# Band attention in pieces of 32 queries and 38 keys, with a unit's scores in one step and its sums over keys in another

## The chip, the cores and the metric

The kernel runs on one core of one Trainium2 chip. The metric is the device time of one execution in microseconds; times are compared as medians of several runs. The profile comes from one further execution that the hardware profiler recorded. TensorE (PE, with its weight loads as PEld) multiplies, VectorE (DVE), ScalarE (ACT) and GpSimd (POOL) do the rest, and SyncE (SP) issues the transfers.

## The reference

A block of attention feeds two feed-forward blocks. For each of 4 batches and 8 heads, of 576 positions and 64 channels, the attention is a sum of two softmaxes: one over the sequence averaged in fours (144 positions, its result repeated four times), and one over a band of seven keys around each query.

```python
q_d = q.reshape(B, H, Sd, factor, D).mean(axis=3)      # factor = 4; k_d, v_d alike
out_up = np.repeat(sm_attn(q_d, k_d, v_d), factor, axis=2)
mask = np.abs(pos[:, None] - pos[None, :]) < factor
scores = np.where(mask, scale * np.matmul(q, k.transpose(0, 1, 3, 2)), -1000000000.0)
attn = np.exp(scores - np.max(scores, axis=-1, keepdims=True))
attn = attn / (np.sum(attn, axis=-1, keepdims=True) + 1e-09)
x = out_up + np.matmul(attn, v)                         # to 2304 tokens x 512
x = (((x @ w1) * (x @ w2)) @ w3) @ w_out
h = x @ w_in;  out = (h / (1 + np.exp(-h))) @ moe2_w_out
```

## The kernel before

The work is one program for one core, written as Python loops that emit instructions; a scheduler may move an instruction on its engine past others that it does not depend on, so the order on an engine is near to the order in the code but not the same.

**Attention** is done in 16 units of two heads (one in partitions 0 to 63, the other in 64 to 127). A unit has these parts, and the letters are also the names of the tiles in the profile. D1 makes the scores of the averaged sequence (`sd`), D2 transposes the softmaxed ones (`td`), D3 multiplies by the averaged values (`od`, copied to `ods`). L1 makes band scores (`s`) in blocks of 64 queries and 70 keys, adds the mask into `E`, takes the maximum and the softmax; L2 transposes `E` (`tl`, copied to `ET` by ScalarE); L3 multiplies by the values in `vw` (`ol`), adds the averaged part (`xf`) and splits the sum into two float32r parts `x` (a cast on ScalarE and a difference on GpSimd or, in the opening, VectorE). Since a bank of PSUM holds 512 columns and nine blocks of 70 need 630, L1, L2 and L3 run twice a unit, for five blocks and for four (`BLOCKS`). These matmuls are plain float32; each appears as two MATMUL records in the trace, a transpose as one.

**The rest** works on float32 numbers split into two float32r parts, three matmuls for each product. In the opening, weights are loaded as 64-bit numbers (`st`), decoded (`dec`) and split, and w3 times w_out is formed (`wp`). Then, for eight pieces of tokens (320 and 256 a batch), `ab_group` makes the two gated products and `y_group` the output, which goes to DRAM. The second feed-forward block (`h`, `g`, `o`) takes the last third of the time.

**The order.** The steps of attention stand in a list `steps`; `run_steps(n)` runs them up to the n-th. In the opening a list of events with due times mixes them with the decoding and `wprime`; later one call after each slot (a slot is one `ab_group` or half a `y_group`, 12 matmuls on the whole array) lets a step or so go in. Before, a unit has nine steps, so that each of D1, L2, L1, L3, D2, L1, L2, D3, L3 stands between two slots:

```python
n = 36 + max(0, i - 3) if i < 40 else 72 + ((i - 39) * 36) // 46   # steps due after slot i
```

PSUM has four banks for `mm` tiles (`ab`, `y`, `wp`), two with the tag T (`td`, `tl`, `od`, `ol`) and two with the tag S (`sd`, `s`). `ab_group` of a batch reads `x` of its four units, the fourth unit's last. The built program gives each matmul the part of TensorE's 128x128 array that just holds its rows (32, 64 or 128) and output columns: 128x128 for `ab`, `y`, `td` and `tl`, 64x64 for `sd` and `s`, 128x64 for `od` and `ol`.

Of the kernel before, what the change touches and what calls it, by code (L numbers as in the profile page):

```python
# [19 lines left out]
QB, KW, NQB = 64, 70, 9  # L20
BLOCKS = ((0, 1, 2, 3, 4), (5, 6, 7, 8))
SD = S // 4
# [10 lines left out]
def tile_model(ctx: ExitStack, tc: tile.TileContext, qk, vw, vr, w12, w3t, wo, wb, out):  # L33
# [33 lines left out]
    mask = cst.tile([P, 6, KW], F32, name="mask")  # L67
    nc.gpsimd.memset(mask, 0.0)
    for e in range(2):
        mv = mask[64 * e:64 * e + 64]  # L70
        nc.gpsimd.affine_select(
            out=mv, in_=mv, compare_op=ALU.is_ge, fill=NEG, base=0,
            pattern=[[0, 6], [1, KW]], channel_multiplier=-1,
        )
        nc.gpsimd.affine_select(
            out=mv, in_=mv, compare_op=ALU.is_ge, fill=NEG, base=6,
            pattern=[[0, 6], [-1, KW]], channel_multiplier=1,
        )
    nc.gpsimd.memset(mask[:, 0, 0:3], NEG)
    nc.gpsimd.memset(mask[:, 5, KW - 3:KW], NEG)  # L80
# [103 lines left out]
    def load_vw(u):  # L184
        if u >= NU:
            return
        t = att.tile([80, NQB, P], F32, tag="vw", name=f"vw{u}", bufs=1)
        nc.sync.dma_start(t, vw[u // 4, u % 4])
        A["vw", u] = t
# [8 lines left out]
    def pool_qk(u):  # L198
        if u >= NU:
            return  # L200
        t = att.tile([P, 2, SD], F32, tag="qkd", name=f"qkd{u}", bufs=2)
        src = A["qk", u].rearrange("p (t c) -> p t c", t=2)[:, :, :S]
        src = src.rearrange("p t (s r) -> p t s r", r=4)
        nc.vector.tensor_reduce(out=t, in_=src, axis=AX.X, op=ALU.add)
        A["qkd", u] = t
# [10 lines left out]
    def softmax(src, E, m, n, width, scale, gain):  # L216

        z = att.tile([P, 16], F32, tag="sm", name="sm")
        nb, sv = z[:, 0:n], z[:, 8:8 + n]
# [97 lines left out]

    def L2(u, h):
        E = A.pop(("E", u, h))
        n = len(BLOCKS[h])  # L320
        ET = att.tile([KW, 5, P], F32, tag="ET", name=f"ET{u}_{h}")
        for j0, j1 in ((0, n // 2), (n // 2, n)):
            tp = t_tile(f"tl{u}_{h}_{j0}")
            for j in range(j0, j1):
                nc.tensor.transpose(tp[:KW, (j - j0) * P:(j - j0 + 1) * P], E[:, j, :], ident)  # L325
            nc.scalar.copy(
                ET[:, j0:j1, :].rearrange("p j q -> p (j q)"), tp[:KW, :(j1 - j0) * P]
            )
        A["ET", u, h] = ET
# [3 lines left out]
    def L3(u, h):  # L333
        ET = A.pop(("ET", u, h))
# [139 lines left out]
    events += [(0.2 + i, 2, i) for i in range(36)]  # L474
# [155 lines left out]
    for i, slot in enumerate(slots):  # L630
# [9 lines left out]
        run_steps(36 + max(0, i - 3) if i < 40 else 72 + ((i - 39) * 36) // 46)  # L640
# [141 lines left out]
```

## Time and profile before

| | |
|---|---|
| median of 3 runs | 947.56 us (945.53 to 948.35) |
| profiled execution | 947.99 us, span 946.2 us, mean granted TensorE clock 0.978 |
| TensorE, matmul / weight load | busy 892.4 us (94%) / 802.3 us (85%) |
| VectorE / ScalarE / GpSimd | busy 459.7 / 317.1 / 258.0 us |
| opening, 0 to about 172 us | TensorE waits in it, VectorE is the fullest engine |
| gated products with attention, to about 436 us | TensorE without gaps |
| gated products without attention, then the second block | TensorE nearly without gaps |

The span runs from the first to the last instruction. Busy time is the union of an engine's instructions; matmuls are pipelined and their ends modelled, so what a group costs is better read from the starts of its neighbours than from its own length.

### The profile page before, as it was taken

What the parts mean: (1) busy time and instruction counts of PE and PEld (TensorE: products, weight loads), DVE (VectorE), ACT (ScalarE), POOL (GpSimd) and SP (SyncE); (2) the same over time, 40 slices, a digit from 0 to 9 for tenths busy, and PEclk for the clock granted to TensorE, in tenths of its full rate; (3) what the DMA queues carried; (4) which work ended last, traced back from release to release, by engine and by line L of the source; (5) the groups of instructions that cost most, each with busy time, mean ns of one, the idle gap of its engine ahead of it and who ended that gap; (6) DMA issues with size and microseconds to landing.
All of it is one profiled execution on the core that took longest, in us unless ns stands there. A gap on an engine that the chain in (4) does not pass through costs nothing.

```text
span 946.2 us, 15978 instructions
## 1 busy us (share of the span) xinstructions
PE 892.4 (94%) x6224; PEld 802.3 (85%) x6224; DVE 459.7 (49%) x997; ACT 317.1 (34%) x966; POOL 258.0 (27%) x269
## 2 busy tenths in 40 slices
PE   5767789999999999999999998999999999999998
PEld 4545578899989999999999897989989989999897
DVE  7888999635453444324637999222221221222221
ACT  6466675443333333334224533211211211111111
POOL 1000014434243333324112154422422423322221
PEclk9787999999999999999999999999999999999999
DMA  8555544221422121121512544200200000000000
GB/s 272 167 179 182 185 132 127 63 76 56 139 78 77 58 72 53 31 68 40 178 65 75 185 139 133 63 6 1 68 1 1 34 1 1 34 1 1 35 1 34
DMA packets 26285, 73.58 MB, mean 78 GB/s; under 512 B 2912, under 2 KB 10080, under 8 KB 26208
## 3 DMA queue, kind: packets, MB, share of 16 engines
q1 hardware_dynamic: 26208, 72.54, 24.3%
q8 instruction: 49, 0.80, 0.4%
q14 instruction: 28, 0.23, 0.1%
HBM read 63.09 MB, written 9.44 MB: 77 GB/s over the span
## 4 chain that ended last, share of the span: by engine, by line
PE 73%; DVE 12%; DMA 6%; ACT 4%; issue 3%; POOL 1%; SPq 0%; DVEq 0%; ACTq 0%; POOLq 0%
PE o L697 19%; PE h L670 19%; PE ab L500 18%; PE y L533 9%; DVE dec L142 3%; DMA st<-wb 3%; DVE dec L147 2%; DMA st<-w3t 2%; PE ol L341 1%; PE s L300 1%; DVE dec L133 1%; DMA st<-w 1%; DVE dec L137 1%; PE tl L325 1%; ACT dec L123 1%
## 5 line engine op out<-in xcount | busy, mean ns | idle before, releaser
L681 POOL TENSOR_TENSOR g<-gf,g 128x384 fp32r<-128x384 f32 x96 | 104.8, 1092 | 275.9 <-DVE g L680 275.9
L678 DVE TENSOR_TENSOR gf<-h,sg 128x384 f32<-128x384 f32 x96 | 53.4, 556 | 258.7 <-ACT sg L676 258.7
L676 ACT ACTIVATE sg<-h 128x384 f32<-128x384 f32 x96 | 47.0, 491 | 290.3 <-PE h L670 290.3
L500 PE MATMUL ab<-x,w_wA 128*128 128x320 f32 (+1 forms) x768 | 112.7, 300 | 0.8 <-DVE w_wA L160 0.8
L500 PE MATMUL ab<-x,w_wB 128*128 128x320 f32 (+1 forms) x768 | 113.2, 300 | 0.0
L533 PE MATMUL y<-c,w_wC 128*128 128x320 f32 (+1 forms) x768 | 111.2, 299 | 0.0
L500 PEld LDWEIGHTS ab<-x,w_wA 128*128 128x128 f32 x768 | 103.2, 188 | 4.4 <-issue 2.0
L500 PEld LDWEIGHTS ab<-x,w_wB 128*128 128x128 f32 x768 | 103.6, 188 | 2.6 <-issue 0.8
L533 PEld LDWEIGHTS y<-c,w_wC 128*128 128x128 f32 x768 | 102.9, 188 | 2.7 <-issue 1.6
L518 POOL TENSOR_TENSOR c<-cf,c 128x320 fp32r<-128x320 f32 (+1 forms) x64 | 54.8, 856 | 140.2 <-DVE c L517 120.5
L407 PE MATMUL wp<-w_wA,w_w 128*128 128x512 f32 x192 | 63.4, 477 | 13.1 <-ACT w_w L159 12.0
L123 ACT ACTIVATE dec<-st 128x512 f32<-128x512 f32 x72 | 48.4, 674 | 69.9 <-DMA st<-wb 30.9
L224 ACT ACTIVATE E<-E,sm 128x70 f32<-128x70 f32 x144 | 49.0, 342 | 49.0 <-DVE sm L220 49.0
L407 PEld LDWEIGHTS wp<-w_wA,w_w 128*128 128x128 f32 x192 | 41.4, 228 | 24.9 <-ACT w_w L159 14.1
L514 DVE TENSOR_TENSOR cf<-ab,af 128x320 f32<-128x320 f32 (+1 forms) x64 | 29.0, 453 | 66.3 <-PE ab L500 60.1
L697 PE MATMUL o<-w_wA,g 128*128 128x512 f32 x216 | 55.7, 401 | 4.2 <-POOL g L681 3.6
L670 PE MATMUL h<-yhl,w_wC 128*128 128x384 f32 x288 | 55.2, 341 | 0.0
L670 PE MATMUL h<-yhl,w_wB 128*128 128x384 f32 x288 | 54.2, 337 | 0.5 <-ACT yo L542 0.5
L670 PE MATMUL h<-yhl,w_wA 128*128 128x384 f32 x288 | 54.4, 337 | 0.0
L697 PE MATMUL o<-w_wB,g 128*128 128x512 f32 x216 | 54.2, 395 | 0.0
L697 PE MATMUL o<-w_wC,g 128*128 128x512 f32 x216 | 54.1, 395 | 0.0
L670 PEld LDWEIGHTS h<-yhl,w_wC 128*128 128x128 f32 x288 | 52.0, 191 | 2.2
(92 smaller groups left out, 1377.6 us busy)
## 6 DMA issues: line engine op xcount, KB each, us to landing
st<-wb SPq DMA_DIRECT2D x32, 512.0 KB, 4.1
qk<-qk SPq DMA_DIRECT2D x16, 579.0 KB, 3.8
st<-w3t SPq DMA_DIRECT2D x16, 512.0 KB, 5.2
st<-w SPq DMA_DIRECT2D x16, 512.0 KB, 4.6
vw<-vw SPq DMA_DIRECT2D x16, 360.0 KB, 3.7
vr<-vr SPq DMA_DIRECT2D x16, 320.0 KB, 3.2
st<-ydram SPq DMA_DIRECT2D x12, 384.0 KB, 3.3
out<-os SPq DMA_DIRECT2D x18, 256.0 KB, 2.1
```

The source lines that it names most:

```text
L123: nc.scalar.activation(v.bitcast(F32), st[:, :, 1].bitcast(F32), AF.Abs)
L224: nc.scalar.activation(E[:, j, :], src[:, j, :], AF.Exp, bias=nb[:, j:j + 1], scale=scale, accum_out=sv[:, j:j + 1],)
L407: nc.tensor.matmul(acc, lhsT=w3v[:, a, k, j * P:(j + 1) * P], rhs=wov[:, b, k, :], start=(gp == 0 and k == 0 and n == 0), stop=(gp == 3 an ...
L500: nc.tensor.matmul(acc[:, :N], lhsT=wv[:, i, w, kk, :], rhs=x[:, j, :], start=(n == 0), stop=(n == 11),)
L514: nc.vector.tensor_tensor(out=cf, in0=acc[:, :N], in1=C.pop("af"), op=ALU.mult)
L518: nc.gpsimd.tensor_tensor(out=c[:, 1], in0=cf, in1=c[:, 0].bitcast(F32), op=ALU.subtract)
L533: nc.tensor.matmul(acc[:, :N], lhsT=WP[kf // 2][:, i, kf % 2, ec * P:(ec + 1) * P], rhs=c[:, j, :], start=(kf == 0 and n == 0), stop=(kf = ...
L670: nc.tensor.matmul(acc[:, :TT], lhsT=w[:, i, kk, :], rhs=y[:, j, kk, :], start=(n == 0), stop=(n == 11),)
L676: nc.scalar.activation(sg, acc[:, :TT], AF.Sigmoid)
L678: nc.vector.tensor_tensor(out=gf, in0=acc[:, :TT], in1=sg, op=ALU.mult)
L681: nc.gpsimd.tensor_tensor(out=g[:, 1], in0=gf, in1=g[:, 0].bitcast(F32), op=ALU.subtract)
L697: nc.tensor.matmul(acc_ps[t][j], lhsT=g[:, a, j * P:(j + 1) * P], rhs=w[:, b, 512:1024], start=(f == 0 and n == 0), stop=(f == 15 and n == 2),
```

## The change

The band is cut into pieces of 32 queries and 38 keys instead of 64 and 70. A block of 64 queries of a head has two pieces, so a unit has four strips of 32 partitions (`g`: two heads, two halves) by nine columns of 38 keys: 342 columns, which fit one bank. L1 therefore runs once a unit (36 matmuls of 32x38 instead of 18 of 64x70), and mask, maximum and softmax once for all. L2 transposes nine times 38 columns, in three T banks of three instead of four of two or three. L3 still fills two banks, with 36 matmuls of 64x32 that contract 38 keys instead of 18 of 64x64 that contract 70; the values come as 18 windows of 38 keys (`vw`, 40 partitions). The built program gives `s` parts of 64x32 (four strips), `ol` 64x64, and `tl`, which now writes 38 partitions, 128x64.

The list has three steps a unit: `scores` (D1, L1), `turn` (D2, L2, the averaging of the next unit) and `sums` (D3, L3, L3), in the order scores(u), sums(u-1), turn(u); the calls run a third as many. `qkd`, `E` and `ET` have one buffer each instead of two.

```diff
-    def L1(u, h):
-        t = A["qk", u]
-        n = len(BLOCKS[h])
-        sp = s_tile(f"s{u}_{h}")
-        for j, i in enumerate(BLOCKS[h]):
-            for e in range(2):
-                r = slice(64 * e, 64 * e + 64)
-                nc.tensor.matmul(
-                    sp[r, j * KW:(j + 1) * KW],
-                    lhsT=t[r, i * QB:(i + 1) * QB], rhs=t[r, S + i * QB:S + i * QB + KW],
+    def L1(u):
+        t = A.pop(("qk", u))
+        sp = s_tile(f"s{u}")
+        for i in range(NQB):
+            for g in (0, 2, 1, 3):
+                r = slice(64 * (g // 2), 64 * (g // 2) + 64)
+                q0 = 64 * i + QW * (g % 2)
+                nc.tensor.matmul(
+                    sp[QW * g:QW * g + QW, i * KW:(i + 1) * KW],
+                    lhsT=t[r, q0:q0 + QW], rhs=t[r, S + q0:S + q0 + KW],
                     start=True, stop=True,
                 )
-        if h == 1:
-            A.pop(("qk", u))
-        Et = att.tile([P, 5, KW], F32, tag="E", name=f"E{u}_{h}")
-        E = Et[:, :n, :]
-        m = att.tile([P, 5], F32, tag="ml", name=f"ml{u}_{h}")[:, :n]
+        E = att.tile([P, NQB, KW], F32, tag="E", name=f"E{u}", bufs=1)
+        m = att.tile([P, NQB], F32, tag="ml", name=f"ml{u}")
         nc.vector.tensor_tensor(
-            out=E, in0=sp[:, :n * KW].rearrange("p (j w) -> p j w", j=n),
-            in1=mask[:, 2 * h:2 * h + n, :], op=ALU.add,
+            out=E, in0=sp[:, :NQB * KW].rearrange("p (j w) -> p j w", j=NQB), in1=mask, op=ALU.add
         )
         nc.vector.tensor_reduce(out=m, in_=E, axis=AX.X, op=ALU.max)
-        A["E", u, h] = E
-        softmax(E, E, m, n, KW, 0.125, 1.0)
-
-    def L2(u, h):
-        E = A.pop(("E", u, h))
-        n = len(BLOCKS[h])
-        ET = att.tile([KW, 5, P], F32, tag="ET", name=f"ET{u}_{h}")
-        for j0, j1 in ((0, n // 2), (n // 2, n)):
-            tp = t_tile(f"tl{u}_{h}_{j0}")
-            for j in range(j0, j1):
-                nc.tensor.transpose(tp[:KW, (j - j0) * P:(j - j0 + 1) * P], E[:, j, :], ident)
+        A["E", u] = E
+        softmax(E, E, m, NQB, KW, 0.125, 1.0)
...
+    def L2(u):
+        E = A.pop(("E", u))
+        ET = att.tile([KW, NQB, P], F32, tag="ET", name=f"ET{u}", bufs=1)
+        for j0 in range(0, NQB, 3):
+            tp = t_tile(f"tl{u}_{j0}")
+            for j in range(3):
+                nc.tensor.transpose(tp[:KW, j * P:(j + 1) * P], E[:, j0 + j, :], ident)
...
         for j, i in enumerate(BLOCKS[h]):
-            for e in range(2):
+            for g in (0, 2, 1, 3):
+                e, sub = divmod(g, 2)
                 r = slice(64 * e, 64 * e + 64)
...
+                c0 = 64 * j + QW * sub
+                nc.tensor.matmul(
+                    op[r, c0:c0 + QW], lhsT=v[:KW, 2 * i + sub, r],
+                    rhs=ET[:, i, QW * g:QW * g + QW], start=True, stop=True,
                 )
...
+    def scores(u):
+        D1(u)
+        L1(u)
+        load_qk(u + 2)
+
+    def turn(u):
+        D2(u)
+        L2(u)
+        pool_v(u)
+        load_vr(u + 1)
+        pool_qk(u + 1)
+
+    def sums(u):
+        D3(u)
+        L3(u, 0)
+        L3(u, 1)
+        load_vw(u + 1)
+
     steps = []
     for u in range(NU):
-        steps.append(lambda u=u: D1(u))
+        steps.append(lambda u=u: scores(u))
         if u:
-            steps.append(lambda u=u: L2(u - 1, 1))
-        steps.append(lambda u=u: L1(u, 0))
-        if u:
-            steps.append(lambda u=u: (L3(u - 1, 1), load_vw(u)))
-        steps.append(lambda u=u: (D2(u), pool_v(u), load_vr(u + 1)))
-        steps.append(lambda u=u: (L1(u, 1), load_qk(u + 2)))
-        steps.append(lambda u=u: (L2(u, 0), pool_qk(u + 1)))
-        steps.append(lambda u=u: D3(u))
-        steps.append(lambda u=u: L3(u, 0))
-    steps.append(lambda: L2(NU - 1, 1))
-    steps.append(lambda: L3(NU - 1, 1))
+            steps.append(lambda u=u: sums(u - 1))
+        steps.append(lambda u=u: turn(u))
+    steps.append(lambda: sums(NU - 1))
...
-    events += [(0.2 + i, 2, i) for i in range(36)]
+    events += [(0.2 + 2.8 * i, 2, i) for i in range(13)]
...
-        run_steps(36 + max(0, i - 3) if i < 40 else 72 + ((i - 39) * 36) // 46)
+        n = 36 + max(0, i - 3) if i < 40 else 72 + ((i - 39) * 36) // 46
+        run_steps(n // 3 + 1)
```

How this moves TensorE's instructions is seen at three places. A row is line, operation, output<-inputs, stationary columns x moving columns, and how many follow each other. The first place is in the first batch's gated products, where the averaged and band results of unit 5 are made (`od5`, `ol5`) between bundles of `y`. Before:

```order
L285 MATMUL od5_1931<-EdT5_1831,vd5_1844 64x144 x4
L533 MATMUL y0_0_0_1918<-c0_0_4_1617,w_wC_1229 128x320 x3
L533 MATMUL y0_0_0_1918<-c0_0_5_1690,w_wC_1229 128x320 x3
L533 MATMUL y0_0_0_1918<-c0_0_6_1754,w_wC_1247 128x320 x3
L533 MATMUL y0_0_0_1918<-c0_0_7_1828,w_wC_1247 128x320 x3
L341 MATMUL ol5_0_1953<-ET5_0_1906,vw5_1811 64x64 x10
L533 MATMUL y0_0_1_1969<-c0_0_0_1352,w_wC_737 128x320 x3
```

After, the sums of that unit:

```order
L547 MATMUL y0_0_1_2176<-c0_0_7_2001,w_wC_1426 128x320 x3
L288 MATMUL od5_2204<-EdT5_2004,vd5_2033 64x144 x4
L341 MATMUL ol5_0_2211<-ET5_2017,vw5_1947 64x32 x20
L341 MATMUL ol5_1_2237<-ET5_2017,vw5_1947 64x32 x16
L547 MATMUL y0_0_2_2261<-c0_0_0_1543,w_wC_880 128x320 x3
```

`od` and both `ol` now follow each other, with twice as many matmuls of half the columns, where each stood between bundles of 12.

The second place is the transposing of the band part in the same stretch. Before, the second half of unit 5 (`tl5_1`):

```order
L533 MATMUL y0_0_1_1969<-c0_0_6_1754,w_wC_1247 128x320 x3
L533 MATMUL y0_0_1_1969<-c0_0_7_1828,w_wC_1247 128x320 x3
L325 MATMUL tl5_1_0_2016<-ident_82,E5_1_1873 70x128 x2
L325 MATMUL tl5_1_2_2020<-ident_82,E5_1_1873 70x128 x2
L533 MATMUL y0_0_2_2024<-c0_0_0_1352,w_wC_737 128x320 x3
```

After, the turn of unit 6, with the averaged part's `td6` ahead of it:

```order
L547 MATMUL y0_0_3_2289<-c0_0_3_1708,w_wC_891 128x320 x3
L271 MATMUL td6_0_2303<-ident_82,Ed6_2093 72x128 x3
L271 MATMUL td6_1_2309<-ident_82,Ed6_2093 72x128 x3
L547 MATMUL y0_0_3_2289<-c0_0_4_1749,w_wC_1415 128x320 x2
L323 MATMUL tl6_0_2316<-ident_82,E6_2141 38x128 x3
L323 MATMUL tl6_3_2321<-ident_82,E6_2141 38x128 x3
L547 MATMUL y0_0_3_2289<-c0_0_4_1749,w_wC_1415 128x320
L547 MATMUL y0_0_3_2289<-c0_0_5_1874,w_wC_1415 128x320
L323 MATMUL tl6_6_2326<-ident_82,E6_2141 38x128 x3
L547 MATMUL y0_0_3_2289<-c0_0_5_1874,w_wC_1415 128x320 x2
```

The two transposed banks of `td` are followed, two big matmuls on, by two of `tl`, and after two more by the third; before, `td` and each half of `tl` stood in slots of their own.

The third place is the first reader of batch 1, `ab1_0_0_0`, which ends with `x7_0`, made from `ol7_0`. Before, its rows begin right behind these:

```order
L341 MATMUL ol7_0_2525<-ET7_0_2473,vw7_2378 64x64 x10
L500 MATMUL ab0_1_7_0_2541<-x0_1_485,w_wA_1633 128x256 x3
L500 MATMUL ab0_1_7_0_2541<-x1_1_814,w_wA_1633 128x256 x3
L500 MATMUL ab0_1_7_0_2541<-x2_1_1116,w_wA_1633 128x256 x3
L500 MATMUL ab0_1_7_0_2541<-x3_1_1478,w_wA_1633 128x256 x3
L251 MATMUL sd8_2556<-qkd8_2483 64x144 x6
L500 MATMUL ab0_1_7_1_2574<-x0_1_485,w_wA_1633 128x256 x3
L500 MATMUL ab0_1_7_1_2574<-x1_1_814,w_wA_1633 128x256 x3
L500 MATMUL ab0_1_7_1_2574<-x2_1_1116,w_wA_1633 128x256 x3
L500 MATMUL ab0_1_7_1_2574<-x3_1_1478,w_wA_1633 128x256 x3
L325 MATMUL tl7_1_0_2593<-ident_82,E7_1_2440 70x128 x2
L325 MATMUL tl7_1_2_2597<-ident_82,E7_1_2440 70x128 x2
```

After:

```order
L288 MATMUL od7_2827<-EdT7_2617,vd7_2646 64x144 x4
L341 MATMUL ol7_0_2834<-ET7_2630,vw7_2564 64x32 x20
L341 MATMUL ol7_1_2860<-ET7_2630,vw7_2564 64x32 x16
L514 MATMUL ab1_0_0_0_2884<-x4_0_1922,w_wB_802 128x320 x3
L514 MATMUL ab1_0_0_0_2884<-x5_0_2234,w_wB_802 128x320 x3
L514 MATMUL ab1_0_0_0_2884<-x6_0_2539,w_wB_802 128x320 x3
L514 MATMUL ab1_0_0_0_2884<-x7_0_2857,w_wB_802 128x320 x3
```

The two bundles of `ab0_1_7` that stood between `ol7_0` and its reader are gone ahead; only `ol7_1` is between.

## Rows read from the trace of the kernel before

**Rows 1.** Busy us by stretch: PE, PEld, DVE, ACT, POOL; clock, DMA share, GB/s.

```profile
0.00:172.00 172.00, 131.02 (x945) 101.35 (x946) 151.14 (x330) 104.68 (x321) 19.22 (x28) 0.89 0.54 171
178.00:436.00 258.00, 256.51 (x2502) 238.33 (x2501) 104.15 (x269) 97.88 (x413) 88.68 (x108) 1.00 0.23 71
600.00:946.20 346.20, 342.47 (x1709) 308.37 (x1707) 78.46 (x166) 51.03 (x99) 96.86 (x89) 1.00 0.06 19
```

**Rows 2.** TensorE in order of time: start us, us, line, operation, out<-in, count.

```profile
179.46 2.00 PE L533 MATMUL y<-c,w_wC 128*128 128x320 f32 x12
181.40 0.71 PE L285 MATMUL od<-EdT,vd 72*64 72x144 f32 x8
182.04 2.02 PE L533 MATMUL y<-c,w_wC 128*128 128x320 f32 x12
183.99 0.80 PE L341 MATMUL ol<-ET,vw 70*64 70x64 f32 x20
184.72 2.03 PE L533 MATMUL y<-c,w_wC 128*128 128x320 f32 x12
186.68 0.95 PE L251 MATMUL sd<-qkd 64*64 64x144 f32 x12
187.56 2.03 PE L533 MATMUL y<-c,w_wC 128*128 128x320 f32 x12
189.43 0.60 PE L325 MATMUL tl<-ident,E 128*70 128x128 f32 x4
189.78 2.01 PE L533 MATMUL y<-c,w_wC 128*128 128x320 f32 x12
191.72 0.83 PE L300 MATMUL s<-qk 64*64 64x70 f32 x20
192.48 2.03 PE L533 MATMUL y<-c,w_wC 128*128 128x320 f32 x12
194.44 0.69 PE L341 MATMUL ol<-ET,vw 70*64 70x64 f32 x16
195.05 2.03 PE L533 MATMUL y<-c,w_wC 128*128 128x320 f32 x12
196.92 0.82 PE L268 MATMUL td<-ident,Ed 128*72 128x128 f32 x6
197.49 2.00 PE L533 MATMUL y<-c,w_wC 128*128 128x320 f32 x12
...
467.33 14.24 PE L500 MATMUL ab<-x,w_wA 128*128 128x320 f32 x96
481.41 0.75 PE L500 MATMUL ab<-x,w_wB 128*128 128x256 f32 x5
```

**Rows 3.** Weight loads of whole-array and of s matmuls: busy us, mean ns.

```profile
L500 PEld LDWEIGHTS ab<-x,w_wB 128*128 128x128 f32 x768 | 103.6, 188 | 2.6 <-issue 0.8 <-DVE w_wC L422 0.2
L300 PEld LDWEIGHTS s<-qk 64*64 64x64 f32 x576 | 22.7, 143 | 13.0 <-issue 4.3 <-DVE E L310 3.7 <-ACT Ed L224 3.6
```

**Rows 4.** ScalarE in order of time, first and last copy of td.

```profile
197.45 0.37 ACT L272 COPY EdT<-td 72x256 f32<-72x256 f32 x1 [1.05 <-PE td L268]
198.06 0.20 ACT L275 COPY EdT<-td 72x32 f32<-72x32 f32 x1
```

**Rows 5.** From ol to x: VectorE's add and GpSimd's difference, 320 columns.

```profile
L352 DVE TENSOR_TENSOR xf<-ol,ods 128x320 f32<-128x320 f32 x16 | 7.8, 486 | 12.8 <-PE ol L341 12.7
L363 POOL TENSOR_TENSOR x<-xf,x 128x320 fp32r<-128x320 f32 x12 | 10.7, 891 | 20.9 <-ACT x L362 20.6
```

**Rows 6.** VectorE's groups of the band softmax in the first 172 us.

```profile
L310 DVE TENSOR_TENSOR E<-s,mask 128x350 f32<-128x350 f32 (+1 forms) x11 | 5.3, 478 | 0.0
L314 DVE TENSOR_REDUCE ml<-E 128x5 f32<-128x350 f32 (+1 forms) x10 | 4.7, 470 | 0.0
L230 DVE TENSOR_SCALAR sm<-sm 128x3 f32<-128x3 f32 (+2 forms) x15 | 3.8, 255 | 3.4 <-ACT E L224 2.5 <-ACT Ed L224 0.8
L233 DVE RECIPROCAL sm<-sm 128x3 f32<-128x3 f32 (+2 forms) x15 | 2.6, 172 | 0.0
```

More of the change, by code (lines that the diff above doesn't have):

```diff
@@ L19 @@
 OFF = (0, 320)
-QB, KW, NQB = 64, 70, 9
+NQB, QW, KW = 9, 32, 38
 BLOCKS = ((0, 1, 2, 3, 4), (5, 6, 7, 8))
@@ L66, in tile_model @@
     make_identity(nc, ident)
-    mask = cst.tile([P, 6, KW], F32, name="mask")
+    mask = cst.tile([P, NQB, KW], F32, name="mask")
     nc.gpsimd.memset(mask, 0.0)
-    for e in range(2):
-        mv = mask[64 * e:64 * e + 64]
+    for g in range(4):
+        mv = mask[QW * g:QW * g + QW]
         nc.gpsimd.affine_select(
             out=mv, in_=mv, compare_op=ALU.is_ge, fill=NEG, base=0,
-            pattern=[[0, 6], [1, KW]], channel_multiplier=-1,
+            pattern=[[0, NQB], [1, KW]], channel_multiplier=-1,
         )
@@ L76, in tile_model @@
             out=mv, in_=mv, compare_op=ALU.is_ge, fill=NEG, base=6,
-            pattern=[[0, 6], [-1, KW]], channel_multiplier=1,
+            pattern=[[0, NQB], [-1, KW]], channel_multiplier=1,
         )
-    nc.gpsimd.memset(mask[:, 0, 0:3], NEG)
-    nc.gpsimd.memset(mask[:, 5, KW - 3:KW], NEG)
+    for e in range(2):
+        nc.gpsimd.memset(mask[64 * e:64 * e + 32, 0, 0:3], NEG)
+        nc.gpsimd.memset(mask[64 * e + 32:64 * e + 64, NQB - 1, KW - 3:KW], NEG)
     W = {}
@@ L186, in load_vw @@
             return
-        t = att.tile([80, NQB, P], F32, tag="vw", name=f"vw{u}", bufs=1)
+        t = att.tile([40, 2 * NQB, P], F32, tag="vw", name=f"vw{u}", bufs=1)
         nc.sync.dma_start(t, vw[u // 4, u % 4])
@@ L200, in pool_qk @@
             return
-        t = att.tile([P, 2, SD], F32, tag="qkd", name=f"qkd{u}", bufs=2)
+        t = att.tile([P, 2, SD], F32, tag="qkd", name=f"qkd{u}", bufs=1)
         src = A["qk", u].rearrange("p (t c) -> p t c", t=2)[:, :, :S]
@@ L216, in softmax @@
     def softmax(src, E, m, n, width, scale, gain):
-        z = att.tile([P, 16], F32, tag="sm", name="sm")
-        nb, sv = z[:, 0:n], z[:, 8:8 + n]
+        z = att.tile([P, 2 * NQB], F32, tag="sm", name="sm")
+        nb, sv = z[:, 0:n], z[:, NQB:NQB + n]
         nc.vector.tensor_scalar(out=nb, in0=m, scalar1=-scale, scalar2=None, op0=ALU.mult)
@@ L326, in L2 @@
             nc.scalar.copy(
-                ET[:, j0:j1, :].rearrange("p j q -> p (j q)"), tp[:KW, :(j1 - j0) * P]
+                ET[:, j0:j0 + 3, :].rearrange("p j q -> p (j q)"), tp[:KW, :3 * P]
             )
-        A["ET", u, h] = ET
+        A["ET", u] = ET
     X = {}
     def L3(u, h):
-        ET = A.pop(("ET", u, h))
+        ET = A["ET", u]
         v = A["vw", u]
@@ L338, in L3 @@
         for j, i in enumerate(BLOCKS[h]):
-            for e in range(2):
+            for g in (0, 2, 1, 3):
+                e, sub = divmod(g, 2)
                 r = slice(64 * e, 64 * e + 64)
+                c0 = 64 * j + QW * sub
                 nc.tensor.matmul(
-                    op[r, j * QB:(j + 1) * QB], lhsT=v[:KW, i, r], rhs=ET[:, j, r],
-                    start=True, stop=True,
+                    op[r, c0:c0 + QW], lhsT=v[:KW, 2 * i + sub, r],
+                    rhs=ET[:, i, QW * g:QW * g + QW], start=True, stop=True,
                 )
@@ L346, in L3 @@
             A.pop(("vw", u))
+            A.pop(("ET", u))
         if u == NU - 1 and h == 1:
@@ L747 @@
     )
-    vw = np.zeros((B, H // 2, 80, NQB, 2 * D), v.dtype)
-    for i in range(NQB):
-        vw[:, :, :KW, i] = vp[:, :, QB * i:QB * i + KW]
+    vw = np.zeros((B, H // 2, 40, 2 * NQB, 2 * D), v.dtype)
+    for i in range(2 * NQB):
+        vw[:, :, :KW, i] = vp[:, :, QW * i:QW * i + KW]
     vr = np.zeros((B, H // 2, 80, 2, 4, 2 * D), v.dtype)
```

## Prediction

> **What bounds the kernel now.** I read the busy time by stretch first [rows 1]. In the last 346.2 us TensorE is busy for 342.5; nothing of the change runs there, so that stage only shifts. From 178 to 436 us, where the attention of units 4 to 15 is strewn between the gated matmuls, TensorE is busy 256.5 of 258 us at full clock (1.00, the 2.4 GHz level), VectorE only 104 and ScalarE 98: a microsecond more or less of TensorE time there is a microsecond of the kernel. In the first 172 us the fullest engine is VectorE (151 of 172); TensorE has 131 with waits in it.
>
> The order of time on TensorE then prices each attention group [rows 2]. The reader is to subtract: a group between two bundles of 12 big matmuls costs the distance of the bundles' starts less 12 big matmuls. One big matmul of 320 columns takes 0.147 us (96 of them from 467.33 to 481.41), so 12 take 1.76. That gives: od 182.04-179.46-1.76 = 0.82; ol of five blocks 184.72-182.04-1.76 = 0.92; sd 1.08; tl of four 0.46; s of five blocks 0.94; ol of four 0.81; td 0.68. (By the split below, s of four is 0.82 and tl of five 0.55.) A unit of before thus costs 7.1 us of TensorE.
>
> These prices split. A float32 matmul appears as two records, so ten matmuls are x20. ol: 20 records 0.92, 16 records 0.81, so 0.029 us a record and a rest of 0.34. s of 70 columns: with that same rest 0.60/20 = 0.030 a record. sd and od, 144 columns: (0.82-0.34)/8 and (1.08-0.34)/12, 0.061 a record. The transposes td and tl (the whole array, one record each) cost 0.11 a record and no rest. So each group of matmuls that uses only part of the array pays 0.34 us around it, whatever is in it, and its records follow the moving columns (144/70 = 2.06, 0.061/0.030 = 2.03), about 0.42 ns a column and record.
>
> **The change part by part, in the stretch that TensorE bounds.** Counts are of the order of both programs from the first ab group on.
>
> Group costs. Before: 73 partial-array groups (13 ol of 8, 12 ol of 10, 12 od, 11 sd, 24 s), 73 x 0.34 = 24.8. After: 11 of sd with s, 12 that begin with od, 3 ol alone, and 24 groups of transposes: tl now writes 38 partitions, so it gets a 128x64 piece of the array, where the 70 of before got all of it. 50 x 0.34 = 17.0. Inside the joined groups the piece changes 23 times (sd to s, od to ol); no row shows a change from one piece to another; between 0 and the 0.34 of going out and back I take 0.14, since it is one change and not two: 3.2. Sum **-4.6**.
>
> Scores. Before 432 records at 0.030 = 13.0; after 11 units x 72 = 792 records of 38 columns (the twelfth moved ahead of the first ab group). If the four 32-column strips run abreast as the two halves do now, a record costs 38 x 0.42/2 = 0.008, with a little dispatch 0.0095: 7.5. If only two run abreast, 0.018: 14.3. If records can't follow each other faster than now, 0.029: 23. I take four, as the rows show two pieces abreast both where they share the rows of the array (ol) and where they do not (s), at one price per column. **-5.5**; bounds -5.5 and +10.
>
> Sums over keys (L3). The pieces halve the moving columns (64 to 32) but not the 64 columns of weights, and double the loads: 448 records become 896. By columns alone a record would cost 0.014: 12.5, -0.5. But a load of 128 columns lasts 188 ns and one of 64 lasts 143 [rows 3]: 0.7 ns a column, some 45 ns for 64 columns, against 32 x 0.84 = 27 ns of moving columns in the same half. The load, not the columns, then sets the pace, which stays near 0.029: 26.0 against 13.0. **+13.0**; bounds -0.5 and +13.
>
> Transposes: as many of them, with 128 moving columns as before, 0.11 each: **0**. That price is of the whole array; no row has a transpose in a part of it. Upper bound: two records each, as any other float32 matmul here: 108 x 0.11 = +11.8. The Trainium skill (TensorEngine Tiling (Array Packing), Restrictions) says that column tiling disables the transpose mode for float32 input. By that rule the sum would be the upper bound; by the rows it stays 0. No run here shows it yet.
>
> Waits inside a step. Now td and tl share two "T" banks in one go. After td begins at 196.92 its four copies start at 197.45 and end at 198.26 [rows 4], so both banks are free 1.34 us after td begins. td (0.66), two big matmuls, the way into the new piece (0.1) and three transposes put tl's second bank at about 1.4: just in time. ScalarE may be busy with something else; I take 0.25 a unit, **+3** (0 to 10). The sums' third bank waits for the copy of od, covered by 1.2 us of L3 records.
>
> X of batch 1. In the order of before ol7_0 stands 12 rows ahead of ab1_0_0_0, its first reader; now ol7_1 alone is between. From ol7_0 to the reader's last quarter there remain ol7_1 (0.93), its exit (0.34) and nine big matmuls (1.32): 2.6 us, against an add of 0.49, a cast of about as much and the GpSimd difference of 0.89 [rows 5], 1.9 plus hand-overs and queues. **+1** (0 to 2.5).
>
> Sum of this stretch: -4.6 - 5.5 + 13 + 0 + 3 + 1 = **+6.9**.
>
> **The opening.** Per unit the mask add and the maximum are one operation instead of two each, of 342 elements against means of 478 and 470 ns [rows 6], and three small ones go (0.16 to 0.26 each): 0.45 + 0.45 + 0.6 = 1.5 us of VectorE. Some 4.5 units lie there: 6.7 us. VectorE is busy 88% of this stretch but shares the chain with transfers and ScalarE; I credit half, **-3.3** (0 to -10). ScalarE's exponentials are as many as before; the load queue's order hardly moves.
>
> Sum: +3.6. The profiled execution took 947.99 us (span 946.2), so **951.6**; it lay 0.4 above the median of the runs, 947.56, which is less than this sum can resolve. Within 0.3% (2.8 us) a measurement can't tell it from no change.
>
> **The rivals.**
> (a) The transposes lose their one-record form in the smaller piece. For it: the piece does change. Against: they are still marked as transposes in the program. Price +11.8: 963.4. The skill's sentence above is what speaks for it; chance 0.2.
> (b) The four strips don't run abreast: +6.8 (two) to +15.5 (pace of now): 958.4 to 967.1. For it: no row shows more than two abreast. The Trainium skill (TensorE: Matmul & The Clock Gate, Wait — 56ns, not 53.3ns?) puts the floor between starts at about 25 ns; by that the scores would be 792 x 0.025 = 19.8, 12.3 above my value; the rows here have nothing below 0.029 a record and can't tell. Chance 0.2.
> (c) The other side: L3's loads are hidden and its records follow the columns, 13.5 off: 938.1. It decides once a load of 64 columns takes under about 30 ns. Against it stand rows 3. Chance 0.1.
> (d) The opening gives back all of VectorE's savings and its waits on transfers shrink as well: -10 instead of -3.3: 944.9. For it the 88%; against it that the loads, not VectorE, end many waits there. Chance 0.08.
>
> My own case keeps 0.42, with +-5 from the waits and the opening: by itself 0.17 faster, 0.38 same, 0.45 slower, range 946 to 957. Faster: 0.42 x 0.17 + nearly all of (c) and most of (d) = 0.21. Same: 0.16 + some of (b) and (d) = 0.21. Slower: the rest, 0.58. Range of all: (c) is left out below, (a) and half of (b) held above: 942 to 966.
>
> **What would show it.** Start to start in the second stretch, less the big matmuls: sd with s 0.34+0.73+0.14+0.68 = 1.9 us (2.5 or 3.3 under b); od with ol 0.34+0.49+0.14+2.1 = 3.1 (1.9 under c); the turn with its six and three transposes 0.66+0.68+0.99 = 2.3 plus waits (3.3 under a). L323 should count 144 records (288 under a), L303 and L341 1152 each. VectorE's busy time in the opening should fall by some 6 us, and the first big matmul at full pace come a few microseconds earlier. I am wrong if the opening moves by more than the whole second stretch, or if TensorE there shows idle time where I count none.

## The result: faster by 0.9%, where 0.4% slower was forecast

| | before | after |
|---|---|---|
| median (range) of 10 runs each on one chip | 946.73 us (943.73 to 948.35) | 938.76 us (933.56 to 940.61) |
| ratio | | 0.9909, 95% interval 0.9886 to 0.9931 |
| profiled execution, span, mean clock | 947.99, 946.2, 0.978 | 940.48, 938.7, 0.969 |
| first matmul of `y` | 179.46 us | 172.60 us |
| first `y` to first `h` (529.88 and 524.14) | 350.4 | 351.5 |
| first `h` to the end (code unchanged) | 416.3 | 414.6 |

8.0 us less by the medians, 7.5 between the profiled executions: 6.9 in the opening, -1.1 between the first `y` and the first `h`, and 1.8 in the second block. The last is no effect that I can tie to the change: in the kernels below the same code took 412.6 to 414.3.

Busy time by stretch after, for [rows 1] (PE, PEld, DVE, ACT, POOL; clock, DMA share, GB/s):

```profile
0.00:172.00 172.00, 137.63 (x1397) 111.87 (x1398) 148.08 (x316) 109.06 (x354) 23.97 (x36) 0.87 0.56 177
172.00:430.00 258.00, 257.92 (x3243) 243.77 (x3242) 83.89 (x214) 93.89 (x392) 81.42 (x97) 0.98 0.24 69
592.50:938.70 346.20, 342.45 (x1714) 308.73 (x1712) 80.13 (x168) 52.21 (x100) 97.44 (x89) 1.00 0.06 19
```

The second line is the one to stop at: TensorE is as full as before, but its granted clock is 0.98 where it was 1.00. It falls three times there. Two windows of 4 us each around the first two falls show where (the clock is the third number from the end):

```profile
248.00:252.00 4.00, 4.00 (x86) 3.51 (x82) 4.00 (x9) 0.35 (x1) 1.86 (x2) 0.95 0.32 86
252.00:256.00 4.00, 4.00 (x20) 4.00 (x19) 0.55 (x1) 0.85 (x3) 3.00 (x3) 0.63 0.82 215
...
276.00:280.00 4.00, 4.00 (x85) 3.76 (x82) 1.49 (x5) 0.82 (x3) 1.50 (x3) 0.86 0.27 73
280.00:284.00 4.00, 4.00 (x25) 4.00 (x25) 0.97 (x2) 0.54 (x2) 3.60 (x4) 0.71 0.41 101
```

Each pair adds up to about 3.4 us at the lower level (1.2 GHz; windows of 2 us within show 0.50), so 1.7 us of work lost: (0.05 + 0.37) x 4 and (0.14 + 0.29) x 4; the third fall, between 328 and 336 us, shows 0.76 and 0.81, (0.24 + 0.19) x 4. TensorE was never idle ahead of them. What it did is in its order of time (start us, us, ..., count), here ahead of the second fall:

```profile
275.64 0.71 PE L288 MATMUL od<-EdT,vd 72*64 72x144 f32 x8
276.28 2.29 PE L341 MATMUL ol<-ET,vw 38*64 38x32 f32 x72
278.50 3.27 PE L514 MATMUL ab<-x,w_wA 128*128 128x320 f32 x12
281.56 3.33 PE L514 MATMUL ab<-x,w_wB 128*128 128x256 f32 x24
```

A whole sums step, and right behind it twelve big matmuls that take 3.06 us instead of 1.76. The other two falls lie behind the sums of 247.7 and 326.6 in the same way; other sums steps have no fall behind them.

The groups, for [rows 2], where the clock is whole:

```profile
176.12 5.55 PE L547 MATMUL y<-c,w_wC 128*128 128x320 f32 x36
181.59 0.71 PE L288 MATMUL od<-EdT,vd 72*64 72x144 f32 x8
182.24 2.29 PE L341 MATMUL ol<-ET,vw 38*64 38x32 f32 x72
184.45 5.55 PE L547 MATMUL y<-c,w_wC 128*128 128x320 f32 x36
189.84 0.82 PE L271 MATMUL td<-ident,Ed 128*72 128x128 f32 x6
190.42 0.54 PE L547 MATMUL y<-c,w_wC 128*128 128x320 f32 x2
190.92 0.82 PE L323 MATMUL tl<-ident,E 128*38 128x128 f32 x6
191.49 0.55 PE L547 MATMUL y<-c,w_wC 128*128 128x320 f32 x2
191.97 0.51 PE L323 MATMUL tl<-ident,E 128*38 128x128 f32 x3
192.23 1.42 PE L547 MATMUL y<-c,w_wC 128*128 128x320 f32 x8
193.49 3.00 PE L514 MATMUL ab<-x,w_wB 128*128 128x256 f32 x24
196.41 0.95 PE L254 MATMUL sd<-qkd 64*64 64x144 f32 x12
197.30 0.85 PE L303 MATMUL s<-qk 64*32 64x38 f32 x72
198.07 4.53 PE L514 MATMUL ab<-x,w_wB 128*128 128x256 f32 x36
```

Read as in the prediction, start of one bundle to start of the next less the big matmuls (0.147 us for 320 columns, 0.119 for 256): sums 184.45 - 176.12 - 36 x 0.147 = 3.04 (forecast 3.1); scores 198.07 - 192.23 - 8 x 0.147 - 24 x 0.119 = 1.81 (1.9); the turn (`td`, six and three of `tl`) 0.68 + 0.78 + 0.45 = 1.91 (2.33 and 0.25 of waits). A unit costs 6.8 us of TensorE; it was 7.1. The counts, over the whole execution:

```profile
L341 PE MATMUL ol<-ET,vw 38*64 38x32 f32 x1152 | 39.3, 224 | 6.7 <-DVE ods L293 6.7
L323 PE MATMUL tl<-ident,E 128*38 128x128 f32 x144 | 23.3, 293 | 2.0 <-ACT EdT L278 1.5 <-ACT ET L324 0.4
L303 PE MATMUL s<-qk 64*32 64x38 f32 x1152 | 14.6, 205 | 0.0
```

VectorE in the first 172 us, for [rows 6] (busy us, mean ns):

```profile
L310 DVE TENSOR_TENSOR E<-s,mask 128x342 f32<-128x342 f32 x6 | 3.0, 506 | 0.0
L313 DVE TENSOR_REDUCE ml<-E 128x9 f32<-128x342 f32 x6 | 3.0, 502 | 0.0
...
L236 DVE RECIPROCAL sm<-sm 128x3 f32<-128x3 f32 (+1 forms) x12 | 2.2, 184 | 0.0
L233 DVE TENSOR_SCALAR sm<-sm 128x3 f32<-128x3 f32 (+1 forms) x12 | 1.9, 162 | 0.8 <-ACT Ed L227 0.8
```

Mask add and maximum take 6.0 us instead of 11.3 (12 operations of each up to the first `y`; [rows 6] stops at 172 us and has 10.0), the small operations less too. Up to the first `y`, before and after:

```profile
0.00:179.46 179.46, 137.03 (x1002) 106.88 (x1003) 156.32 (x344) 109.16 (x343) 23.31 (x33) 0.90 0.53 167
0.00:172.60 172.60, 138.23 (x1402) 112.47 (x1403) 148.08 (x316) 109.06 (x354) 23.97 (x36) 0.87 0.56 176
```

VectorE was busy 8.2 us less, and the first `y` came 6.9 us earlier.

### The profile page after: what moved, and what is told of

It reads as the page before. It is cut to its first block, busy times and chain, and to the rows that moved or that the text cites. A ratio compares the mean times of both kernels' runs of the same rounds, so it can differ in the third digit from the quotient of the medians.

```text
span 938.7 us, 18154 instructions
## 1 busy us (share of the span) xinstructions
PE 894.7 (95%) x7376; PEld 813.8 (87%) x7376; DVE 433.2 (46%) x918; ACT 313.5 (33%) x959; POOL 251.6 (27%) x261
## 4 chain that ended last, share of the span: by engine, by line
PE 78%; DVE 11%; DMA 4%; ACT 4%; issue 3%; POOL 1%; SPq 0%; DVEq 0%; ACTq 0%; POOLq 0%
PE ab L514 20%; PE o L712 19%; PE h L685 19%; PE y L547 10%; PE ol L341 3%; DVE dec L145 2%; DVE dec L150 2%; PE tl L323 2%; DMA st<-wb 2%; PE wp L421 2%; DMA st<-wo 2%; PE sd L254 1%; DVE dec L136 1%; PE s L303 1%; DVE dec L140 1%
## 5 line engine op out<-in xcount | busy, mean ns | idle before, releaser
L514 PEld LDWEIGHTS ab<-x,w_wB 128*128 128x128 f32 x768 | 107.2, 194 | 2.1 <-DVE w_wC L436 0.9
L547 PE MATMUL y<-c,w_wC 128*128 128x320 f32 (+1 forms) x768 | 108.0, 298 | 0.0
L514 PEld LDWEIGHTS ab<-x,w_wA 128*128 128x128 f32 x768 | 107.5, 197 | 0.5
L421 PE MATMUL wp<-w_wA,w_w 128*128 128x512 f32 x192 | 60.0, 467 | 11.2 <-ACT w_w L162 11.2
L521 ACT COPY af<-ab 128x320 f32<-128x320 f32 (+1 forms) x64 | 25.1, 396 | 85.6 <-PE ab L514 85.6
```

The lines of the kernel that those rows point to most:

```text
L421: nc.tensor.matmul(acc, lhsT=w3v[:, a, k, j * P:(j + 1) * P], rhs=wov[:, b, k, :], start=(gp == 0 and k == 0 and n == 0), stop=(gp == 3 an ...
L514: nc.tensor.matmul(acc[:, :N], lhsT=wv[:, i, w, kk, :], rhs=x[:, j, :], start=(n == 0), stop=(n == 11),)
L547: nc.tensor.matmul(acc[:, :N], lhsT=WP[kf // 2][:, i, kf % 2, ec * P:(ec + 1) * P], rhs=c[:, j, :], start=(kf == 0 and n == 0), stop=(kf = ...
```

## The experiments

| kernel | median us (range) | ratio to before (95%) | first `y` | `y` to `h` | falls there |
|---|---|---|---|---|---|
| after | 938.76 (933.56 to 940.61) | 0.9909 (0.9886 to 0.9931) | 172.6 | 351.5 | 3 |
| VectorE work back | 945.74 (944.14 to 948.6) | 0.9996 (0.9978 to 1.0015) | 176.6 | 353.5 | 4 |
| fine steps | 937.73 (936.72 to 941.45) | 0.9900 (0.9877 to 0.9923) | 171.4 | 352.0 | 0 |
| whole-array `tl` | 937.52 (935.07 to 944.13) | 0.9898 (0.9868 to 0.9929) | 168.1 | 351.6 | 3 |
| L3 in strips | 928.51 (926.3 to 930.61) | 0.9802 (0.9777 to 0.9828) | 167.1 | 343.4 | 2 |
| v and x on GpSimd | 943.33 (938.92 to 947.89) | 0.9967 (0.9945 to 0.9990) | 173.7 | 355.0 | 5 |
| L1 strip by strip | 956.59 (954.26 to 957.16) | 1.0106 (1.0072 to 1.0140) | 172.6 | 368.3 | 4 |
| sums split | 933.26 (932.67 to 935.41) | 0.9870 (0.9832 to 0.9909) | 166.5 | 350.4 | 0 |
| strips, v and x on GpSimd | 932.94 (930.57 to 937.72) | 0.9864 (0.9833 to 0.9896) | 178.5 | 344.8 | 2 |
| strips, sums split | 929.82 (925.66 to 931.79) | 0.9793 (0.9760 to 0.9825) | 173.6 | 342.5 | 0 |
| strips, fine steps | 922.84 (922.47 to 923.17) | 0.9735 (0.9708 to 0.9762) | 164.6 | 343.6 | 0 |

The last three columns are of one profiled execution each (of `strips, v and x on GpSimd` it was the slowest of the six, 937.72); "falls" are those of the granted clock between first `y` and first `h`. The theory: the opening follows VectorE's work, and the second stretch gains less than its instructions say because the clock answers to the joined steps. The rival: order and joining gave the gain.

**VectorE work back.**

```diff
-        nc.vector.tensor_reduce(out=m, in_=E, axis=AX.X, op=ALU.max)
+        for _ in range(4 if opening[0] else 1):
+            nc.vector.tensor_reduce(out=m, in_=E, axis=AX.X, op=ALU.max)
```

> The changed kernel, with the maximum over a unit's scores taken four times instead of once while the opening lasts (three more VectorE operations of 0.50 us a unit; the result is the same). Theory A, the first big matmul of the y groups comes 6.9 us earlier after the change because VectorE sets the pace of the opening and the change took work off it: 1.5 us back in each of about 5 units is 7.5, so the first y matmul returns from 172.6 to about 180 us and the time from 938.8 to about 946. Rival B, the opening gained by the order of the steps or by their joining, and VectorE has room: first y at 172 to 174, time 939 to 940.

The gain is gone: 945.7. Up to its first `y`, for the two lines above:

```profile
0.00:176.58 176.58, 136.22 (x1402) 109.37 (x1403) 154.26 (x331) 110.36 (x354) 24.90 (x36) 0.86 0.54 173
```

15 operations more, 6.2 us more of VectorE, the first `y` 4.0 later in these two executions, and the median 7.0 higher; 2.0 of that lies between `y` and `h`, with a fourth fall of the clock. The first `y` did not go back to 180 as expected, so one for one is too much; but more than half is passed on (4.0 of 6.2), and with VectorE's work restored the new order of the steps gains nothing that can be measured. The chain of work that ended last says the same of the opening. Up to the first `y` it ran over VectorE for 81 us before, 60 after the change and 73 with the work back; the rest of it is TensorE (15, 53 and 45), ScalarE (33, 29 and 32), transfers (34, 18 and 15) and time in which the engine waited for nothing that the profile shows. So VectorE has the largest part of this chain in these three kernels, and never the whole of it.

**Fine steps** (code cut; seven steps of a unit, apart as they were before, with the new pieces).

```diff
-        steps.append(lambda u=u: scores(u))
+        steps.append(lambda u=u: D1(u))
+        steps.append(lambda u=u: (L1(u), load_qk(u + 2)))
...
-        run_steps(n // 3 + 1)
+        run_steps(7 * n // 9 + 2)
```

> The new pieces (32 queries, 38 keys, one bank) in the fine steps of the kernel before: D1, L1, D2, L2, D3 and the two halves of L3 each in a step of its own, with big matmuls between. Theory A: the opening's lead is VectorE's and stays (first y at 172 to 174 us). In the second stretch od, ol and s pay their way in and out again: 0.2 for sd and s, 0.2 for od and ol, 0.34 for the two ol, 0.74 us a unit, over 11 units +8. The granted clock falls three times in that stretch of the changed kernel (251, 278 and 330 us, some 1.7 us lost each), each time behind a sums step of 3 us of small matmuls. If the long step is what the clock answers to, the falls go (-5) and the time is about 942; if they have nothing to do with it, about 947. Rival B, order and joining gave the opening's lead: first y near 179, time 949 to 954.

No fall of the clock, the opening's lead stays, the second stretch within 0.5 us of the changed kernel's: apart, `sd` costs 1.08 and `s` 0.98 in its timeline, 0.25 a unit more than joined, the sums 0.48 more and the turn 0.12 less (both below), so joining saves TensorE some 6 us in 11 units, and loses 5.1 of them through the clock. The clock of the other runs agrees: over the whole execution it was 0.967 to 0.974 in the ten runs of the changed kernel, 0.976 to 0.984 in the six of this one. The time is 4 below the expected 942: the stretch came out 2.5 better, the rest lies ahead of it and behind.

**Whole-array `tl`** (code cut; besides, `E` gets a tenth block of columns, which GpSimd sets to zero once a unit).

```diff
-                nc.tensor.transpose(tp[:KW, j * P:(j + 1) * P], E[:, j0 + j, :], ident)
+                nc.tensor.transpose(tp[:2 * KW, j * P:(j + 1) * P],
+                    E[:, j0 + j:j0 + j + 2, :].rearrange("p j k -> p (j k)"), ident)
```

> The changed kernel, where each transpose of the scores takes two neighbouring blocks (76 columns) instead of one (38), so that it fills 76 partitions and uses the whole array; ScalarE copies the first 38 rows as before. The transposes are as many and move as many columns. Theory A, a transpose in the 128x64 piece costs 0.109 us as in the whole array, and each of the two groups of a turn pays some 0.17 us for its change of piece: six 0.66 instead of 0.84, three 0.33 instead of 0.48, 0.33 us a unit, -3.6 in the second stretch, time about 935. Rival B, the extra 0.17 is a wait for the bank or for E and not for the piece: the groups stay at 0.84 and 0.48, time 938 to 940.

Rival B by the stretch that it is about: `y` to `h` 351.6 against 351.5 (the median, 937.5, lies between the two expectations). So a change of piece for a transpose costs nothing, and my theory of the extra 0.17 fell. It is a wait for the T bank: the counts above name ScalarE's copies out of the T tiles (`EdT`, `ET`) as what `tl` waited for, and the extra goes where `td` and `tl` stand 12 big matmuls apart (strips with fine steps):

```profile
179.10 0.82 PE L271 MATMUL td<-ident,Ed 128*72 128x128 f32 x6
179.68 2.01 PE L552 MATMUL y<-c,w_wC 128*128 128x320 f32 x12
181.52 0.82 PE L323 MATMUL tl<-ident,E 128*38 128x128 f32 x6
182.10 0.54 PE L552 MATMUL y<-c,w_wC 128*128 128x320 f32 x2
```

182.10 - 179.68 - 1.76 = 0.66 is six times 0.11 and nothing else, in the piece of 128x64; two matmuls behind `td` the same group costs 0.78. That the first `y` came 4.5 us earlier in this execution I can't assign: the edit does not touch VectorE's work, and the medians differ by 1.2.

**L3 in strips.**

```diff
-            for g in (0, 2, 1, 3):
-                e, sub = divmod(g, 2)
-                r = slice(64 * e, 64 * e + 64)
+            for sub in range(2):
+                for s in (0, 2, 1, 3):
+                    r = slice(32 * s, 32 * s + 32)
+                    g = 2 * (s // 2) + sub
```

> The changed kernel, where L3 writes strips of 32 partitions, with weights of 32 columns: 72 matmuls (144 records) a unit instead of 36 (72 records), each of 32 moving columns, four strips in turn. Theory A, the 0.029 us a record of L3 is the load of 64 columns, and loads of 32 with four strips abreast go at the 0.0095 of the scores: od with both ol falls from 3.05 us to 0.34+0.49+0.14+1.37 = 2.3, -0.7 a unit, -8 in the second stretch, time about 931. Rival B, strips that share the rows of the array do not run four abreast (the scores' strips share rows only two by two): 144 records at 0.018 or more, 2.6 us and upward, +0.5 a unit or more, +6, time 945 or above.

Theory A (`y` to `h` -8.1):

```profile
176.09 0.71 PE L288 MATMUL od<-EdT,vd 72*64 72x144 f32 x8
176.74 1.45 PE L342 MATMUL ol<-ET,vw 38*32 38x32 f32 x144
178.11 5.55 PE L548 MATMUL y<-c,w_wC 128*128 128x320 f32 x36
```

144 records in 1.37 us from first start to the next bundle, 0.0095 each, where 72 with weights of 64 columns took 2.21, 0.031 each. Twice the matmuls, of the same moving columns, in 0.6 of the time: it was the weights' columns that set L3's pace. Had each matmul held its strip as long as before, twice as many in twice as many strips would have taken the same 2.2 us. That the stretch came out at the expected -8 is partly luck: the cheaper L3 is worth some 9 us and one fall less 1.7, while TensorE now stands 2 to 3 us in waits around three of the sums.

**L1 strip by strip.**

```diff
-        for i in range(NQB):
-            for g in (0, 2, 1, 3):
+        for g in range(4):
+            for i in range(NQB):
```

> The changed kernel with the 36 matmuls of L1 in another order: nine blocks in one strip of 32 partitions, then the nine of the next, so that neighbours never lie in different strips. Nothing else moves. Theory A, the scores' 0.0095 us a record comes of four strips abreast: one strip alone takes 38 columns at 0.84 ns, 0.032 us a record or more, 72 x 0.0225 = +1.6 us a unit, sd with s 3.5 us instead of 1.86, some +18 in the second stretch, 955 to 962 in all (the loads of a strip's next weights may add to it). Rival B, records of 38 columns follow each other at 0.0095 us whatever strip they are in: no change, 936 to 941.

Theory A. The same matmuls, one strip after the other:

```profile
197.96 0.95 PE L254 MATMUL sd<-qkd 64*64 64x144 f32 x12
198.84 2.35 PE L303 MATMUL s<-qk 64*32 64x38 f32 x72
201.12 4.53 PE L514 MATMUL ab<-x,w_wB 128*128 128x256 f32 x36
```

2.28 us for 72 records, 0.032 each, against 0.77 above: neighbours in four strips run abreast, and the order of a loop is worth 15 us of this stretch; the other 1.7 of its 16.7 is one more fall of the clock.

**Sums split** (code cut; the calls run five ninths as many steps as before the change instead of a third).

```diff
-            steps.append(lambda u=u: sums(u - 1))
+            steps.append(lambda u=u: D3(u - 1))
+            steps.append(lambda u=u: L3(u - 1, 0))
+            steps.append(lambda u=u: (L3(u - 1, 1), load_vw(u)))
```

> The changed kernel with the sums in three steps (D3, L3 of the first half, L3 of the second half, big matmuls between); scores and turn stay joined. Theory A, the clock falls of the changed kernel (three in the second stretch, none in the kernel with all steps fine) come of the 3 us of sums in one go: no falls, od and the two ol cost 3.56 instead of 3.05 us a unit, +0.51 x 11 - 5.1, second stretch within 1 us of the changed kernel's, time 937 to 940. Rival B, the joined scores or the spacing of the steps do it: the falls stay, second stretch +5.6, time 943 to 945.

Theory A: no fall, `y` to `h` 350.4 (-1.1). The groups apart:

```profile
208.07 3.10 PE L518 MATMUL ab<-x,w_wA 128*128 128x256 f32 x24
211.10 0.71 PE L288 MATMUL od<-EdT,vd 72*64 72x144 f32 x8
211.74 3.10 PE L518 MATMUL ab<-x,w_wA 128*128 128x256 f32 x24
214.76 1.35 PE L341 MATMUL ol<-ET,vw 38*64 38x32 f32 x40
216.05 1.68 PE L518 MATMUL ab<-x,w_wA 128*128 128x256 f32 x12
217.65 1.12 PE L341 MATMUL ol<-ET,vw 38*64 38x32 f32 x32
218.71 3.79 PE L518 MATMUL ab<-x,w_wB 128*128 128x320 f32 x24
```

0.82 + 1.46 + 1.24 = 3.52 against 3.04 joined (256 columns: 12 x 0.119 = 1.43): 0.48 a unit, 5.3 over 11 units, against three falls of 1.7. All seven kernels with joined sums have two to five falls there, all five with split sums, the one before the change among them, have none. Where they lie is as telling: each of the 23 falls begins between 0.1 us ahead of the end of a sums step and 1.2 us behind it, though such steps end only eleven times in a kernel's 350 us. The rest of this kernel's gain, some 4 us, lies in the opening.

**v and x on GpSimd, alone and with strips** (`side()` gives GpSimd in the opening too).

```diff
-        return nc.vector if opening[0] else nc.gpsimd
+        return nc.gpsimd
```

> The changed kernel, where the sums of v and the low halves of x go to GpSimd in the opening too, as they do later: 2.7 + 1.6 + 3.3 = 7.6 us of VectorE by the rows of the changed kernel up to 172 us. GpSimd is busy 24 of these 172 us. Theory A, VectorE paces the opening one for one (putting 1.5 us a unit back undid the change's lead): 5 to 7.5 us earlier, time 931 to 934. Rival B, VectorE paces it only down to a point where transfers or TensorE take over, or GpSimd, which takes twice VectorE's time for a difference (0.89 us against 0.45), comes late with x: 937 to 941.

> L3 in strips of 32 partitions (which gave 928.5 us) and the sums of v and low halves of x on GpSimd in the opening. Theory A, both gains are of different stretches and add: 922 to 924. Rival B, GpSimd gives nothing or costs: 928 to 931.

Rival B and worse, 4.5 us above the kernels without it both times. 16 operations fewer, and VectorE as busy as ever up to the first `y` (of the first of the two, without strips):

```profile
0.00:173.71 173.71, 137.64 (x1403) 110.04 (x1404) 148.07 (x300) 109.01 (x354) 45.24 (x52) 0.88 0.55 175
```

What filled it up is seen where a moved operation runs (L213, a sum of v, now on GpSimd):

```profile
99.59 1.28 POOL L213 TENSOR_TENSOR vr<-vr 72x512 f32<-72x512 f32 x1 [6.27 <-DMA vr<-vr]
...
99.97 1.18 DVE L136 TENSOR_SCALAR dec<-dec 128x512 f32<-128x512 f32 x1
...
101.50 0.41 DVE L136 TENSOR_SCALAR dec<-dec 128x512 f32<-128x512 f32 x1
```

The same decoding operation takes 1.18 us beside it and 0.41 without. Up to the first `y` the decoding operations of L150, L145 and L136 that overlapped with work of GpSimd took 926, 876 and 727 ns on the mean, the others 683, 683 and 418. GpSimd was at work 45 us instead of 24, and the means of the three lines in the first 172 us rose from 714, 710 and 453 ns to 750, 731 and 495. (The means alone would not show it: L136 has 515 in the fine steps, where nothing was moved.) So VectorE's unmoved operations stretched by about what had been taken off it. The Trainium skill (Perfetto Trace Analysis, Optimizing Scalar/DVE Operations) says that the two share a read port and that moving work between them may not help; the trace agrees.

That makes no gain; it does not make the loss. In these two executions the first kernel loses 1.1 us in the opening and 3.4 behind it, with five falls of the clock instead of three, and the second loses 11.4 in the opening, where transfers hold 32 us of the chain that ended last, against 16 with strips alone. Why the move should cause either is open.

**Strips with the sums split, and with fine steps.**

> L3 in strips of 32 partitions and the sums in three steps (D3, and the two halves of L3), scores and turn joined. Theory A, each keeps its gain: strips take 0.83 us a unit off L3, the split pays 0.51 a unit and gets back the time of the clock falls (two are left with strips alone, 3.4 us) and the 2 us that TensorE stood before the sums there; the opening is as early as with the split sums alone (first y near 166.5 us): 922 to 926. Rival B, the split pays for nothing that the strips had not already saved: 928 to 931.

> L3 in strips of 32 partitions and all seven steps of a unit fine, as in the kernel before. Against the same with only the sums split it pays 0.2 us a unit for sd and s apart and saves 0.16 in the turn, where the transposes no longer wait for their bank: within 1 us of it by the second stretch, 923 to 927. Rival B, the finer spacing of the steps delays the opening, as its first y at 171.4 against 166.5 us says for the plain pieces: 927 to 930.

By the medians the first of the two lies in its rival's range (929.8, in 928 to 931), the second at its theory's (922.8, just below 923 to 927). The second stretch agrees with theory A both times (342.5 and 343.6), but lies as near to strips alone (343.4). The opening decides, and not as expected: the first `y` at 173.6 and at 164.6, the other way round than the second one's rival said. Strips with fine steps are the best kernel here, 2.65% below before and 15.9 us below the change.

## Why the prediction was wrong, step by step

**The step that failed first is "VectorE is busy 88% of this stretch but shares the chain with transfers and ScalarE; I credit half, -3.3".** The saving was sized fairly (6.7, measured 8.2), and VectorE does share the chain that ended last (81 of 179 us before); the half was a choice that no row of the prediction stood behind. Measured, the opening gained 6.9 us with 8.2 off VectorE, and putting 6.2 us back took the gain of the medians away. How much of the 6.9 is VectorE's alone is less sure, since edits that leave its work as it is move the first `y` by as much (see Open). Rival (d), at 0.08, had the right stretch and the right engine; the measured size of the opening, 6.9, lies between its 10 and the forecast's 3.3.

**The second failed step, and the larger one by its size, is the price of a group in the piece of 128x64.** The forecast charged 0.34 for each of 24 `tl` groups, 8.2 us, "so it gets a 128x64 piece of the array". The 0.34 is shown by od, ol, sd and s alone, all two-record matmuls. `tl` in that piece costs 0.11 a record and nothing around it, as `td` does. The group term was -12.8, not -4.6. (It also holds a small slip: 13 + 12 + 12 + 11 + 24 groups are 72, not 73, which is 0.3 us.)

**Unforeseen: the clock.** Three falls, 5.1 us, in a stretch that I read as bound by TensorE at full clock. Without them the stretch would have come out 4.0 us shorter than before, not 1.1 longer. The forecast had no term for what joined small matmuls do to the granted clock, and this miss cancelled part of the other two. One of the prediction's own signs of being wrong came true: the opening moved by more (6.9) than the whole second stretch (1.1).

**Right by their steps.** The scores at 0.0095 a record (measured 0.0107; four abreast, as L1 strip by strip shows), so rival (b) falls. L3 paced by its loads at 0.029 (0.031), so rival (c) falls, and the strips show why. Transposes of one record, 144 of L323 at 0.11 us, so rival (a) falls. Waits in the turn 0.25 a unit: 1.91 less 15 x 0.109 is 0.27. X of batch 1 was charged 1 us and cost none: TensorE shows no wait from 172 to 436 us after the change. Not counted was a wait of 1.5 us before the change, `td` at 267 us for a bank that VectorE's `xf` held, which is gone:

```profile
267.25 0.52 PE L268 MATMUL td<-ident,Ed 128*72 128x128 f32 x3 [1.49 <-DVE xf L352]
```

The trace disagrees with two rules here. The Trainium skill (TensorE: Matmul & The Clock Gate, Wait — 56ns, not 53.3ns?) puts a floor of some 25 ns between starts, which would make 72 records 1.8 us; the row has 0.77 across four strips, and only one strip after the other stays above it (2.28). The Trainium skill (TensorEngine Tiling (Array Packing), Restrictions) says that column tiling disables the transpose mode for float32; L323 keeps one record and its price in the piece of 128x64.

The forecast with the measured terms: 951.6 - 3.6 (opening) - 8.2 (`tl` groups) - 1 (X) - 1.5 (the old wait) + 5.1 (clock) - 1.8 (second block, unexplained) = 940.6; the profiled execution took 940.5. That is closer than the parts are known: the scores and the sums came out 0.03 to 0.1 us a unit below the forecast, some 1 us that stands in no term, and 1.8 us is unexplained.

**Open.** What the clock answers to: each fall follows a joined sums step, but only 23 of the 77 such steps have one. The opening's spread: among kernels with about the same VectorE work (busy 147 to 150 us up to it) the first `y` lies anywhere from 164.6 to 178.5, and no run here separates order, transfers and chance. Both matter more than the 0.3% that a measurement tells apart.

## What to carry to other kernels

Where one engine is the fullest in a stretch but others share its chain, don't halve a saving on it by feel: here 0.64 (put back) to 0.83 (taken off) of it came through. Put the work back to see. A price read from one kind of instruction holds for that kind: before charging it to another, find a row of that other. Small matmuls can be paced by the columns of their weights (L3) instead of their moving columns, and those of the scores ran abreast only when neighbours in the order lay in different strips; and before packing them into one long step, look at the granted clock behind it.

## What the runs showed of the hardware that I had not expected

- Float32 matmuls in four strips of 32 columns follow each other at 0.0095 to 0.011 us a record, also where all four share the rows of the array (`ol` in strips); one strip alone needs 0.032.
- A sums step of some 2 to 3 us of part-array matmuls, with no idle time ahead of it in the changed kernel, can be followed by 3.4 us at half the clock (23 times in the profiled executions of seven kernels); cut in three groups of 0.8 to 1.5 us, with big matmuls between, it never was in this stretch of five.
- A VectorE operation beside GpSimd work can take far longer: 727 instead of 418 ns on the mean for one kind of decoding operation, 926 instead of 683 for another. 21 us more of GpSimd work so ate the 7.6 us that the move had taken from VectorE.
